# Second product of the attention over the block means in one piece per head, another warm-up, and another list of pieces for the start of a fused kernel

## The chip, the cores and the metric

The kernel runs on one core of a Trainium2 chip. The metric is the device time of one execution in microseconds (us), the median of three runs. The engines are TensorE (PE, with PEld for its weight loads), VectorE (DVE), ScalarE (ACT), GpSimd (POOL) and SyncE (SP, which issues the DMAs here).

## What is computed

Three layers run one behind the other on 3072 tokens (4 sequences of 768) of 512 numbers (8 heads of 64). The first is attention in which each query sees the keys less than 16 positions away, and one summary for each block of 32 keys (the maximum of the keys, the mean of the values):

```python
k_sum = k.reshape(B, H, nb, block, D).max(axis=3)
v_sum = v.reshape(B, H, nb, block, D).mean(axis=3)
scores_l = where(|q_pos - k_pos| < 16, scale * q @ k.T, -1e9)
scores_s = scale * q @ k_sum.T + np.log(block)
a = softmax(concat[scores_l, scores_s])
x = a @ concat[v, v_sum]            # then as 3072 x 512
h = x @ w_in                        # 512 -> 2048
g = h * np.cos(h)
x = g @ w_out                       # 2048 -> 512
# then a soft mixture of 8 experts of 4 slots each over all tokens
logits = x @ phi
slot_out[e] = maximum((softmax(logits, 0).T @ x)[e] @ w1[e], 0) @ w2[e]
out = softmax(logits, 1) @ slot_out
```

## The kernel before

The attention works on 24 groups: a group is 256 queries of four heads, in two parts j of two heads (hh) and four blocks u of 64 queries. A block of 64 queries sees KL = 96 keys and NSUM = 24 summaries, so a row of scores S has 120 numbers. For the first four groups (0 to 3, the first 512 tokens) the pieces of a part are: `sc` (scores on PE, L327 against the keys, L330 against the key summaries that `u`, L199, has reduced), `ev` and `mx` (mask and row maximum on DVE, L336 and L344), `ex` (exponentials on ACT, L366), `nm` and `nt` (normalisation, L449, L451, L456), `tr` and `aT` (transposition on PE, L469, and copy out of PSUM on ACT or DVE, L479), and the two products with the values: `av` over the 96 keys and `aw` over the 24 means, both through `first_x` with one product of 64 columns for each block and head (L520). The means `vs` are made on PE (L215) out of the loads `vb`. Then `xh` and `xl` (L536, L540) split x into two halves of a fast PE format.

The second layer runs in 96 slots: 6 blocks of 512 tokens by 16 blocks of 128 of the 2048 inner columns. A slot has twelve products into h (L580, L581, L588), then `p`, `q` (DVE, L600, L604), `n` (the sine on ACT, L608), `r` (DVE, L618) and the split of g (L622, L631); two slots later its products into the output sums (L652 to L675). In the first 16 slots the weights come by DMA (`W`, the buffers raw) and are converted: `ca`, `cb` on ACT (L134, L139), `cc` on DVE (L148), `cd` on POOL (L156), and their high and low halves (L553, L560). The raw buffers of the weights are single: a load waits for the conversion of the weights two before it. The loads of the keys from the fifth pair on share one buffer (`v2`), so each waits for the reduction `u` of the one before. SP has at most eight DMAs under way.

All pieces up to slot 80 are recorded under names by `do`, and `emit` issues them in the order of the hand list `ORDER` on all five engines: an engine meets its instructions in the order in which the list names them, and waits at each for what it needs. `fill` (L895) records products of a matrix of ones (L902, warmth), whose result nobody reads: in the list f1 and f11 stand at the start and f21 and f31 further down, ten products of 128 columns each. After slot 80 only PE and SP are ordered by hand.

Of the kernel before, what the change touches and what calls it, by code (L numbers as in the profile page):

```python
# [23 lines left out]
QB = 64  # L24
NQ = S // QB
WIN, SUMB = 16, 32
KL = QB + 2 * WIN
NSUM = S // SUMB
KC = KL + NSUM
# [6 lines left out]
NFILL = 40  # L36
F0 = 10
# [36 lines left out]
def body(ctx: ExitStack, tc: tile.TileContext, q0, qk, kT, vT, vn, vx, w, phi, ex, cst, out):  # L74
    nc = tc.nc
# [18 lines left out]
    def do(name, fn, *a):  # L94

        if not waiting:
            return fn(*a)
        assert name not in pieces, name
        pieces[name] = (fn, a)
        queue.append(name)  # L100
# [3 lines left out]
    NM = 6 * KC  # L104
    mask = att.tile([128, 6, KC], F32, name="mask", tag="mask", bufs=1)
    ident = const.tile([128, 128], F32, name="ident")
# [4 lines left out]
    ones = const.tile([128, 128], F32, name="ones")  # L111
# [47 lines left out]
    ksums, vsums, grp = {}, {}, {}  # L159
# [6 lines left out]
    def bank(name):  # L166
        pool, tag = place_of[name]
        return pool.tile([128, 512], F32, name=name, tag=tag)
# [33 lines left out]
    def load_vb(b, i):  # L202
        do(f"b{b}_{i}", load_vb_, b, i)
# [46 lines left out]
    def vsum_first():  # L250

        reserve("vs0")
        for i in range(3):
            do(f"vs0_{i}", vsum_f, i)
        do("vt0", vsum_g)
# [158 lines left out]
    def att_exp(pair):  # L414
        do(f"ae{pair}", att_exp_, pair)
# [66 lines left out]
    def att_D(g):  # L482
        if g < 4:
            reserve(f"av{g}")
            for j in range(2):
                do(f"av{g}_{j}", first_av, g, j)
                do(f"aw{g}_{j}", first_aw, g, j)
        else:
            do(f"av{g}", att_av, g, (0, 1))
        do(f"xh{g}", att_xh, g)  # L490
        do(f"xl{g}", att_xl, g)

    def att_av(g, js):
        d = grp[g]
        if "av" not in d:
            d["av"] = bank(f"av{g}") if g < 4 else ps_m.tile([128, 512], F32, name=f"av{g}", tag="m")
        ps = d["av"]
        for j in js:
            for u in range(4):
                c = 256 * j + QB * u  # L500
                for hh in range(2):
                    r = slice(64 * hh, 64 * hh + 64)
                    a = d["aT", j][:, 128 * u + 64 * hh:] if g < 4 else d["aT", hh][:, 256 * j + 64 * u:]
                    nc.tensor.matmul(ps[r, c:c + QB], d["v"][:KC, j, u, r], a[:, 0:QB], start=True, stop=True)  # L504

    def first_av(g, j):
        first_x(g, j, grp[g]["v"][:KL, j], slice(0, KL))

    def first_aw(g, j):
        p = 2 * (g % 2) + j  # L510
        first_x(g, j, vsums[0][KL:KC, p:p + 1, :].to_broadcast([NSUM, 4, 128]), slice(KL, KC))

    def first_x(g, j, v, k):
        d = grp[g]
        if "av" not in d:
            d["av"], d["parts"] = bank(f"av{g}"), 0
        for u in range(4):
            for hh in range(2):
                r = slice(64 * hh, 64 * hh + 64)
                nc.tensor.matmul(d["av"][r, 256 * j + QB * u:256 * j + QB * u + QB], v[:, u, r],  # L520
                                 d["aT", j][k, 128 * u + 64 * hh:128 * u + 64 * hh + QB],
                                 start=d["parts"] == 0 and u == 0, stop=d["parts"] == 3 and u == 3)
        d["parts"] += 1

    def att_x(g):
        b, o = g // 4, 256 * ((g // 2) % 2)
        if b not in xh:
            xh[b] = xres.tile([128, 4, TB], F32R, name=f"xh{b}", tag="xh", bufs=2)
            xl[b] = xres.tile([128, 4, TB], F32R, name=f"xl{b}", tag="xl", bufs=2)
        p = 2 * (g % 2)  # L530
        hi, lo = (x[b][:, p:p + 2, o:o + 256] for x in (xh, xl))
        return hi, lo, grp[g]["av"].rearrange("p (j c) -> p j c", j=2)

    def att_xh(g):
        hi, lo, ps = att_x(g)
        nc.scalar.copy(hi, ps)  # L536
# [8 lines left out]
    def split_w(f, part, eng=None, s=None):  # L545
        nm = "io"[part]
        do(f"{nm}h{f if s is None else s}", split_hi, f, part)
        do(f"{nm}l{f if s is None else s}", split_lo, f, part, eng)
# [344 lines left out]
    warmth = ps_h.tile([128, 512], F32, name="warmth", tag="h")  # L893

    def fill(n):  # L895

        for i in range(0, n, 10):
            do(f"f{i + (n > F0)}", fill_, min(10, n - i))

    def fill_(n):  # L900
        for i in range(n):
            nc.tensor.matmul(warmth[:, 0:128], ones, ones, start=True, stop=True)  # L902
# [5 lines left out]

    def load_mask2(_):
        do("N", load_mask2_)  # L910

    def load_mask2_():
        nonlocal mask2
        mask2 = att.tile([128, 6, KC], F32, name="mask2", tag="mask", bufs=1)
        nc.sync.dma_start(out=mask2[:, 0:4, :].rearrange("p w c -> p (w c)"), in_=cst[:, NM + 468:NM + 468 + 4 * KC])

    mask2 = None

    C = lambda t, o, n: (lambda _: do(f"C{o}", lambda: nc.sync.dma_start(out=t, in_=cst[:, o:o + n])))
    todo = dict(F=lambda _: fill(F0), f=lambda _: fill(NFILL), I=C(ident, NM, 128), M=C(mask.rearrange("p w c -> p (w c)"), 0, NM),  # L920
                A=C(avg, NM + 128, 52), S=C(sel, NM + 180, 288), N=load_mask2, P=lambda _: do("P", lambda: nc.sync.dma_start(out=phis.rearrange("p k s -> p (k s)"), in_=phi)),
                K=load_kraw, Q=load_q_first, W=load_w, B=lambda i: load_vb(0, i), V=load_v, G=load_qk, X=load_vs,
                k=ksum, s=scores, e=exps, v=lambda _: vsum_first(), t=turn, d=att_D, c=convert, c1=conv_1,
                w=lambda f: split_w(f, 0), a=att_K)
    for token in PRE.split():
        n = token.lstrip("FfIMNASPKQWBVGXksevtdcwa")
        todo[token[:len(token) - len(n)]](int(n or 0))


    def late_exp(pair):  # L930
        with tc.issue_after(turn_dve["sin"].ins):
            att_exp(pair)
# [7 lines left out]
    for g in range(4, 24):  # L940
        h0 = HF[g // 2 % 2] + 2 * NF * (g // 4 - 1) if g > 7 else HB[g // 2 % 2]
        h = h0 + OA * (g % 2)
        n = h0 + ON + DN * (g % 2)
        if g < 8:
# [4 lines left out]
            c = n + OC  # L949
            at2(c + OD, att_D, g)  # L950
        else:
            v = n - 14 + OD2
# [3 lines left out]
            c = n + OC2  # L956
# [16 lines left out]
    for b in range(1, B):  # L973
        s = 8 * (3 * b - 2) - 4
        for i in range(8):
            load, use, k = (load_kraw, ksum, 4 * b + i) if i < 4 else (load_vraw, vadd, 4 * b + i - 4)
# [31 lines left out]
    for f in range(NPRE, NF):  # L1008
        c = max(f - CL, 0)
# [9 lines left out]
    def emit():  # L1019
        nonlocal waiting  # L1020
        waiting = False
        names = ORDER.split() or queue
        assert sorted(names) == sorted(queue), set(names) ^ set(queue)
# [329 lines left out]
```

## Time and profile before

| | us |
|---|---|
| median of three runs | 727.8 (727.47 to 728.17) |
| profiled execution | 730.21 |
| span of that execution in the trace | 728.4 |
| PE busy | 711.3 (98% of the span) |
| DVE, ACT, POOL busy | 435.8, 411.5, 406.9 |
| PE's share of the chain that ended last | 92% |

The trace is of one execution: times in it are us from the start of its span, and 1.8 us of the execution lie around the span. Busy time is what an engine spends in instructions; "idle before" an instruction has the one that it waited for behind an arrow, or "issue" where the trace shows none. PEclk is the clock that TensorE was granted, as a share of its full speed. The ends of products on PE are modelled, so that neighbouring rows overlap by some hundredths of a microsecond; a product of 32-bit numbers is two records.

### The profile page before, as it was taken

The numbers are of one execution on the slowest core, as the hardware profiler recorded it, in microseconds if no ns is written. First come the engines' busy times: TensorE is split into PE (matmuls) and PEld (weight loads), VectorE is DVE, ScalarE is ACT, GpSimd is POOL, SyncE is SP. The second block draws the span as 40 slices with busy tenths as digits, with TensorE's granted clock in tenths as the row PEclk, the third lists the DMA queues.
The fourth block names the chain that finished last, engine by engine and source line by source line (L and its number), as shares of the span: only waits on it lengthen the run. The fifth ranks groups of instructions, "written<-read, shape, count | busy, mean of one in ns | idle before, by whom it ended". The sixth has DMA issues, their size and how long they took to land.

```text
span 728.4 us, 13277 instructions
## 1 busy us (share of the span) xinstructions
PE 711.3 (98%) x5260; PEld 560.0 (77%) x5260; DVE 435.8 (60%) x680; ACT 411.5 (56%) x772; POOL 406.9 (56%) x310
## 2 busy tenths in 40 slices
PE   9899999999999999999999999999999999999994
PEld 9878777788887887787888787888787887787453
DVE  5678986974676574776574754674953444334323
ACT  4789997565554654654654754564735445434113
POOL 0756857766465565565673666674577665762000
PEclk9899999999999999999999999999999999999998
DMA  9976856402212301401302201301302822227998
GB/s 345 398 281 249 301 212 230 166 22 76 92 67 77 112 1 54 140 24 43 111 1 74 80 0 35 116 1 43 117 1 87 318 87 87 94 95 269 410 370 295
DMA packets 34862, 101.65 MB, mean 140 GB/s; under 512 B 3440, under 2 KB 13936, under 8 KB 32752
## 3 DMA queue, kind: packets, MB, share of 16 engines
q1 hardware_dynamic: 34800, 100.81, 38.1%
q8 instruction: 41, 0.67, 0.4%
q14 instruction: 21, 0.17, 0.1%
HBM read 92.54 MB, written 6.29 MB: 136 GB/s over the span
## 4 chain that ended last, share of the span: by engine, by line
PE 92%; ACT 4%; DVE 2%; issue 1%; POOL 0%
PE h L580 12%; PE h L581 12%; PE h L588 12%; PE acc L666 10%; PE acc L675 10%; PE acc L667 10%; PE tr L469 3%; PE av L504 3%; PE sc L384 2%; PE acc L652 2%; PE acc L653 2%; PE acc L655 2%; PE yp L1219 2%; PE hp L1173 2%; PE warmth L902 2%; PE av L520 1%
## 5 line engine op out<-in xcount | busy, mean ns | idle before, releaser
L631 POOL TENSOR_TENSOR gl<-a,gh 128x512 fp32r<-128x512 f32 x96 | 129.1, 1345 | 120.4 <-ACT gh L622 62.8
L560 POOL TENSOR_TENSOR wol<-w,woh 128x512 fp32r<-128x512 f32 x96 | 126.4, 1318 | 65.4 <-ACT woh L553 64.1
L580 PE MATMUL h<-xh,wih 128*128 128x512 f32 x384 | 155.4, 405 | 2.8 <-DVE a L618 2.8
L581 PE MATMUL h<-xl,wih 128*128 128x512 f32 x384 | 152.7, 398 | 0.0
L600 DVE TENSOR_SCALAR a<-h 128x512 f32<-128x512 f32 x96 | 66.0, 688 | 128.8 <-PE h L588 76.9
L608 ACT ACTIVATE a<-a,halfpi 128x512 f32<-128x512 f32 x96 | 69.4, 724 | 110.1 <-DVE a L604 109.8
L666 PE MATMUL acc<-woh,gh 128*128 128x512 f32 x320 | 127.4, 398 | 0.0
L667 PE MATMUL acc<-wol,gh 128*128 128x512 f32 x320 | 125.4, 392 | 0.0
L560 POOL TENSOR_TENSOR wil<-w,wih 128x512 fp32r<-128x512 f32 x81 | 106.9, 1323 | 30.0 <-PE h L588 11.4
L588 PE MATMUL h<-xh,wil 128*128 128x512 f32 x384 | 106.8, 401 | 0.0
L618 DVE TENSOR_TENSOR a<-h,a 128x512 f32<-128x512 f32 x96 | 65.9, 688 | 50.1 <-ACT a L608 50.1
L580 PEld LDWEIGHTS h<-xh,wih 128*128 128x128 f32 x384 | 72.3, 188 | 23.1 <-issue 3.7
L675 PE MATMUL acc<-woh,gl 128*128 128x512 f32 x320 | 88.3, 397 | 0.0
L581 PEld LDWEIGHTS h<-xl,wih 128*128 128x128 f32 x384 | 72.5, 189 | 16.0 <-DVE xl L540 0.5
L588 PEld LDWEIGHTS h<-xh,wil 128*128 128x128 f32 x384 | 71.0, 189 | 16.7 <-issue 1.0
L553 ACT CAST woh<-w 128x512 fp32r<-128x512 f32 x96 | 59.4, 619 | 32.1 <-PE acc L675 25.1
L553 ACT CAST wih<-w 128x512 fp32r<-128x512 f32 x96 | 59.3, 618 | 25.2 <-PE h L581 23.1
L622 ACT CAST gh<-a 128x512 fp32r<-128x512 f32 x96 | 58.9, 617 | 24.5 <-PE acc L667 19.1
L666 PEld LDWEIGHTS acc<-woh,gh 128*128 128x128 f32 x320 | 60.1, 188 | 14.4 <-issue 1.3
L667 PEld LDWEIGHTS acc<-wol,gh 128*128 128x128 f32 x320 | 60.2, 188 | 12.9
L675 PEld LDWEIGHTS acc<-woh,gl 128*128 128x128 f32 x320 | 58.8, 188 | 13.1 <-issue 0.6
L604 DVE SCALAR_TENSOR_TENSOR a<-a,h 128x512 f32<-128x512 f32 x96 | 65.5, 682 | 2.2
(156 smaller groups left out, 962.3 us busy)
## 6 DMA issues: line engine op xcount, KB each, us to landing
ex<-in_ex_dram SPq DMA_DIRECT2D x64, 512.0 KB
raw<-in_w_dram SPq DMA_DIRECT2D x16, 1024.0 KB
qk<-in_qk_dram SPq DMA_DIRECT2D x20, 736.0 KB
v<-in_vx_dram SPq DMA_DIRECT2D x24, 512.0 KB
kr<-in_kT_dram SPq DMA_DIRECT2D x16, 384.0 KB
out_dram<-o SPq DMA_DIRECT2D x12, 512.0 KB
vr<-in_vT_dram SPq DMA_DIRECT2D x12, 384.0 KB
v<-vs SPq DMA_DIRECT2D x40, 48.0 KB
```

The lines of the kernel that those rows point to most:

```text
L553: nc.scalar.copy(hi, W[f][:, part, :])
L560: (eng or nc.gpsimd).tensor_tensor(out=lo, in0=W[f][:, part, :], in1=hi, op=ALU.subtract)
L580: nc.tensor.matmul(h, hi[:, c], xh[s // NF][:, t, :], start=t == 0, stop=False)
L581: nc.tensor.matmul(h, hi[:, c], xl[s // NF][:, t, :], start=False, stop=False)
L588: nc.tensor.matmul(h, lo[:, c], xh[s // NF][:, t, :], start=False, stop=t == 3)
L600: nc.vector.tensor_scalar(out=a, in0=h, scalar1=0.25, scalar2=MAGIC, op0=ALU.add, op1=ALU.add)
L608: turn_dve["sin"] = nc.scalar.activation(a, a, AF.Sin, bias=halfpi, scale=-TWO_PI)
L618: nc.vector.tensor_tensor(out=a, in0=h, in1=a, op=ALU.mult)
L631: nc.gpsimd.tensor_tensor(out=gl, in0=a, in1=gh, op=ALU.subtract)
L666: nc.tensor.matmul(acc[t], gh[:, c], hi, start=f == 0, stop=False)
L667: nc.tensor.matmul(acc[t], gh[:, c], lo, start=False, stop=False)
L675: nc.tensor.matmul(acc[t], gl[:, c], hi, start=False, stop=f == NF - 1)
```

## The change

Three things are changed. The second product `aw` takes the four query blocks u of a head at once: two products of 256 columns for a part (one per head) in place of eight of 64, with the transposed probabilities read in strides; there are 16 of them in place of 64. The flags that begin and end the sum follow. The warm-up is four products of 512 columns, three in f0 and one in f1, both at the start, in place of forty of 128 columns, twenty of them further down. And the list `ORDER` is made anew, with 1927 names in place of 1929; the rules that it keeps (what waits for what) are the same. Lines up to 520 stand two lower in the new file.

```diff
-NFILL = 40
-F0 = 10
-ORDER = """kz1 kz3 kz2 kz0 K0 f1 Q0 Q2 K1 C0 Q1 f11 K3 C720 u0 C848 K2 sc0_0 W0 sc2_0 u1 K4 Q3 ev0_0 sc0_1
+ORDER = """zz1 kz0 kz3 kz2 kz1 K0 f0 Q0 K1 C0 C848 Q2 K2 Q1 u0 C720 K3 f1 W0 u1 sc0_0 V0 Q3 sc0_1 ev0_0 b0_0
...
     def first_av(g, j):
-        first_x(g, j, grp[g]["v"][:KL, j], slice(0, KL))
-
-    def first_aw(g, j):
-        p = 2 * (g % 2) + j
-        first_x(g, j, vsums[0][KL:KC, p:p + 1, :].to_broadcast([NSUM, 4, 128]), slice(KL, KC))
-
-    def first_x(g, j, v, k):
         d = grp[g]
         if "av" not in d:
             d["av"], d["parts"] = bank(f"av{g}"), 0
+        d["parts"] += 1
         for u in range(4):
             for hh in range(2):
                 r = slice(64 * hh, 64 * hh + 64)
-                nc.tensor.matmul(d["av"][r, 256 * j + QB * u:256 * j + QB * u + QB], v[:, u, r],
-                                 d["aT", j][k, 128 * u + 64 * hh:128 * u + 64 * hh + QB],
-                                 start=d["parts"] == 0 and u == 0, stop=d["parts"] == 3 and u == 3)
+                nc.tensor.matmul(d["av"][r, 256 * j + QB * u:256 * j + QB * u + QB], d["v"][:KL, j, u, r],
+                                 d["aT", j][:KL, 128 * u + 64 * hh:128 * u + 64 * hh + QB],
+                                 start=d["parts"] == 1 and u == 0, stop=False)
+
+    def first_aw(g, j):
+        d = grp[g]
         d["parts"] += 1
+        for hh in range(2):
+            r = slice(64 * hh, 64 * hh + 64)
+            a = d["aT", j][KL:KC, :].rearrange("p (u h c) -> p u h c", u=4, h=2)[:, :, hh, :]
+            nc.tensor.matmul(d["av"][r, 256 * j:256 * j + 256].rearrange("p (u c) -> p u c", u=4),
+                             vsums[0][KL:KC, 2 * (g % 2) + j, r], a, start=False, stop=d["parts"] == 4)
...
     def fill(n):
-
-        for i in range(0, n, 10):
-            do(f"f{i + (n > F0)}", fill_, min(10, n - i))
+        for i, k in enumerate((3,1,)):
+            do(f"f{i}", fill_, k)
 
     def fill_(n):
-        for i in range(n):
-            nc.tensor.matmul(warmth[:, 0:128], ones, ones, start=True, stop=True)
+        for _ in range(n):
+            nc.tensor.matmul(warmth, ones, ones.unsqueeze(1).to_broadcast([128, 4, 128]), start=True, stop=True)
```

What the list moves is seen in the order of the instructions on an engine. On PE, behind the scores of the first four groups: vs are the means of the values, vb a load that they are made of, aT the transposed probabilities of a group and part, v its values, av the sums, tr a transposition of the probabilities S. Before, the three means stand in a row and the products behind them:

```order
L469 MATMUL tr2_0_422<-ident_88,S2_208 120x128 x4
L215 MATMUL vs0_428<-vb0_0_204,avg_90 32x128 x8
L215 MATMUL vs0_428<-vb0_1_231,avg_90 32x128 x8
L215 MATMUL vs0_428<-vb0_2_227,avg_90 32x128 x8
L520 MATMUL av2_460<-aT2_0_439,v2_237 64x64 x8
L520 MATMUL av2_460<-aT2_1_457,v2_237 64x64 x8
L520 MATMUL av0_486<-aT0_0_391,v0_284 64x64 x8
L520 MATMUL av2_460<-aT2_1_457,vs0_471 64x64 x8
```

And in the new list:

```order
L213 MATMUL vs0_353<-vb0_0_173,avg_90 32x128 x8
L467 MATMUL tr0_1_363<-ident_88,S0_171 120x128 x4
L213 MATMUL vs0_353<-vb0_1_194,avg_90 32x128 x8
L213 MATMUL vs0_353<-vb0_2_200,avg_90 32x128 x8
L512 MATMUL av0_402<-aT0_0_388,v0_150 64x64 x8
L467 MATMUL tr2_0_421<-ident_88,S2_224 120x128 x4
L467 MATMUL tr2_1_427<-ident_88,S2_224 120x128 x4
L522 MATMUL av0_402<-aT0_0_388,vs0_416 64x256 x2
L512 MATMUL av2_442<-aT2_0_434,v2_226 64x64 x8
```

Group 0 comes ahead of group 2, transpositions stand between the products, and the second product is two instructions where it was eight.

On SP, the loads from the first weights on (raw0 to raw4 are the weights, kr the keys, q queries, vb and v values). Before:

```order
L126 DMA raw0_160<-in_w_dram 128x2048
L191 DMA kr4_181<-in_kT_dram 128x768
L273 DMA q3_183<-in_q0_dram 128x512
L208 DMA vb0_0_204<-in_vn_dram 128x2x512
L126 DMA raw1_223<-in_w_dram 128x2048
L208 DMA vb0_2_227<-in_vn_dram 128x2x512
L208 DMA vb0_1_231<-in_vn_dram 128x2x512
L290 DMA v2_237<-in_vx_dram 128x1024
L290 DMA v0_284<-in_vx_dram 128x1024
L191 DMA kr5_387<-in_kT_dram 128x768
L290 DMA v1_389<-in_vx_dram 128x1024
L126 DMA raw2_395<-in_w_dram 128x2048
```

And in the new list:

```order
L124 DMA raw0_129<-in_w_dram 128x2048
L288 DMA v0_150<-in_vx_dram 128x1024
L271 DMA q3_152<-in_q0_dram 128x512
L206 DMA vb0_0_173<-in_vn_dram 128x2x512
L206 DMA vb0_1_194<-in_vn_dram 128x2x512
L206 DMA vb0_2_200<-in_vn_dram 128x2x512
L288 DMA v1_222<-in_vx_dram 128x1024
L288 DMA v2_226<-in_vx_dram 128x1024
L124 DMA raw1_264<-in_w_dram 128x2048
L288 DMA v3_287<-in_vx_dram 128x1024
L189 DMA kr4_292<-in_kT_dram 128x768
L124 DMA raw2_322<-in_w_dram 128x2048
```

The four loads of v stand ahead of the load of the fifth keys, kr4, and raw1 stands behind three of them.

On DVE around the tenth slot (sm and rs are the normalisation of an attention group, S its scores, a8 and a9 the slots' intermediate results). Before:

```order
L148 TENSOR_SCALAR w11_1244<-w11_1244 128x1024
L449 TENSOR_SCALAR sm7_1350<-sm7_1350 128x8
L451 RECIPROCAL rs7_1381<-sm7_1350 128x8
L199 TENSOR_REDUCE ks9_1384<-kr9_1313 128x24
L604 SCALAR_TENSOR_TENSOR a9_1355<-a9_1355,h9_1272 128x512
L618 TENSOR_TENSOR a8_1332<-h8_1226,a8_1332 128x512
```

And in the new list:

```order
L146 TENSOR_SCALAR w11_1193<-w11_1193 128x1024
L600 TENSOR_SCALAR a9_1296<-h9_1195 128x512
L604 SCALAR_TENSOR_TENSOR a9_1296<-a9_1296,h9_1195 128x512
L618 TENSOR_TENSOR a8_1270<-h8_1142,a8_1270 128x512
L447 TENSOR_SCALAR sm7_1256<-sm7_1256 128x8
L449 RECIPROCAL rs7_1321<-sm7_1256 128x8
```

The step L618 of slot 8 stands ahead of the normalisation of group 7 instead of behind it, and the key reduction is no longer between them.

## Rows read from the trace of the kernel before

**Rows 1.** Windows: stretch, us; busy us (instructions) of each engine; PEclk, DMA share, GB/s.
```profile
109.00:660.00 551.00, 550.55 (x3560) 438.67 (x3559) 328.02 (x498) 300.21 (x508) 341.01 (x262) 1.00 0.23 82
80.00:103.00 23.00, 23.00 (x186) 18.15 (x185) 20.62 (x32) 22.76 (x57) 17.92 (x10) 1.00 0.73 263
103.00:109.00 6.00, 4.19 (x12) 3.12 (x11) 5.43 (x8) 5.45 (x9) 2.56 (x2) 0.72 0.51 194
33.30:37.00 3.70, 3.70 (x20) 3.33 (x20) 1.38 (x2) 3.49 (x6) 1.34 (x2) 0.50 0.99 405
713.00:719.30 6.30, 5.11 (x36) 3.63 (x28) 3.75 (x7) 3.39 (x7) 0.00 (x0) 1.00 0.94 316
```

**Rows 2.** PE's timeline, 0 to 42 us: start, us, instruction, count [idle before, releaser].
```profile
1.08 7.31 PE L902 MATMUL warmth<-ones 128*128 128x128 f32 x40 [1.08 <-DVE ones L113]
...
11.82 2.50 PE L902 MATMUL warmth<-ones 128*128 128x128 f32 x20
...
20.48 2.40 PE L902 MATMUL warmth<-ones 128*128 128x128 f32 x20
...
27.23 1.03 PE L520 MATMUL av<-aT,vs 24*64 24x64 f32 x28
30.16 1.14 PE L520 MATMUL av<-aT,vs 24*64 24x64 f32 x20 [1.90 <-issue]
...
33.33 3.67 PE L469 MATMUL tr<-ident,S 128*120 128x128 f32 x16
36.93 2.22 PE L520 MATMUL av<-aT,v 96*64 96x64 f32 x64
39.08 2.08 PE L520 MATMUL av<-aT,vs 24*64 24x64 f32 x64
41.09 0.50 PE L580 MATMUL h<-xh,wih 128*128 128x512 f32 x1
```

**Rows 3.** ACT's waits and DVE's groups of instructions, 0 to 49 us.
```profile
ACT S L366 <- DVE mx L344: 9.3, 2, 8.8
ACT xh L536 <- PE av L520: 6.1, 4, 2.3
...
L199 DVE TENSOR_REDUCE ks<-kr 128x24 f32<-128x768 f32 x7 | 6.5, 934 | 5.5 <-DMA kr<-in_kT_dram 5.5
L336 DVE SCALAR_TENSOR_TENSOR S<-sc,mask 128x480 f32<-128x480 f32 x8 | 5.2, 646 | 2.1 <-PE sc L330 2.1
```

**Rows 4.** ACT's timeline: the first exponential, the first sine, what follows it.
```profile
11.06 0.40 ACT L366 ACTIVATE S<-S,mx 128x120 f32<-128x120 f32 x1 [8.84 <-DVE mx L344]
...
48.10 0.73 ACT L608 ACTIVATE a<-a,halfpi 128x512 f32<-128x512 f32 x1
48.73 0.60 ACT L553 CAST woh<-w 128x512 fp32r<-128x512 f32 x1
```

**Rows 5.** PE's timeline in the last stage: products of 256 columns, and a wait.
```profile
692.68 3.64 PE L1219 MATMUL yp<-ex,hT 128*32 128x256 f32 x64
...
715.43 1.69 PE L1254 MATMUL op<-so,cT 128*128 128x256 f32 x12 [0.92 <-DVE so L1242]
```

**Rows 6.** DMA, 0 to 37 us: the sum, and the loads of weights.
```profile
DMA packets 4215, 13.76 MB, mean 372 GB/s; under 512 B 542, under 2 KB 670, under 8 KB 3570
...
raw<-in_w_dram SPq DMA_DIRECT2D x5, 1024.0 KB
```

**Rows 7.** Timelines of ACT, DVE and PE around the tenth slot.
```profile
101.64 0.72 ACT L608 ACTIVATE a<-a,halfpi 128x512 f32<-128x512 f32 x1
...
100.36 2.32 DVE L449 TENSOR_SCALAR sm<-sm 128x8 f32<-128x8 f32 x1 [0.17 <-ACT S L438]
...
103.65 0.68 DVE L604 SCALAR_TENSOR_TENSOR a<-a,h 128x512 f32<-128x512 f32 x1
104.25 0.68 DVE L618 TENSOR_TENSOR a<-h,a 128x512 f32<-128x512 f32 x1
...
105.08 0.47 PE L580 MATMUL h<-xh,wih 128*128 128x512 f32 x1 [1.81 <-DVE a L618]
```

More of the change, by code (lines that the diff above doesn't have):

```diff
@@ L919, in body @@
     C = lambda t, o, n: (lambda _: do(f"C{o}", lambda: nc.sync.dma_start(out=t, in_=cst[:, o:o + n])))
-    todo = dict(F=lambda _: fill(F0), f=lambda _: fill(NFILL), I=C(ident, NM, 128), M=C(mask.rearrange("p w c -> p (w c)"), 0, NM),
+    todo = dict(f=lambda _: fill(0), I=C(ident, NM, 128), M=C(mask.rearrange("p w c -> p (w c)"), 0, NM),
                 A=C(avg, NM + 128, 52), S=C(sel, NM + 180, 288), N=load_mask2, P=lambda _: do("P", lambda: nc.sync.dma_start(out=phis.rearrange("p k s -> p (k s)"), in_=phi)),
```

2 lines of the change are left out of this document (1 added, 1 removed).

## The prediction

> **What bounds the kernel now.** I began with the windows over stages [rows 1]. From 109 to 660 us TensorE (PE) is busy 550.55 of 551.00 us at a granted clock of 1.00: nothing in the change alters the products of that stretch, so it only starts earlier or later, and whatever the start gains reaches the end one for one. In 80 to 103 us both PE (23.00 of 23.00) and ScalarE (ACT, 22.76 of 23.00) are full. What can be won lies before the first slots of the second layer run, and at one hole at 103 to 109, where PE is busy 4.19 of 6.00 us at 0.72.
>
> The timeline of PE [rows 2] shows the losses of the start: warm-up products at 1.08, at 11.82 and at 20.48; an idle gap of 1.90 us ahead of 30.16 in which PE waited for nothing that the trace shows; then a clock of 0.50 (33.3 to 37.0 in [rows 1]) and the first product of h at 41.09. ACT's waits [rows 3] show who suffers: it waits 6.1 us, four times, for the last products of av before it can cast x (L536). And the timeline of ACT [rows 4] shows where the two meet: its first exponential starts at 11.06 and the first sine of a slot, which every later slot stands behind, at 48.10. Between these ACT has 37.04 us, of which it waits the 6.1 and 0.5 (9.3 in all for maxima, less the 8.84 ahead of the first exponential); so it has 30.4 us of work there and is the chain that I follow.
>
> **The change part by part.** Warm-up at the start: 40 records took 7.31 us, and at the full clock 20 take 2.50 or 2.40, so about .12 us each. 40 of them would be 4.8; the 2.5 us more are some 21 records at half the clock. Now there are 8 records of four times the columns: 21 slow short ones (5.04 us) are 5.25 long ones, the other 2.75 take .48 each, 1.3 us; the sum is 6.4, so they end at 7.4 to 7.5 instead of 8.39. Bounds are 4.9 (all fast) and 8.8 (all slow); I take -0.9 for the first score and so for the first exponential, 10.1 to 10.2.
>
> Warm-up in the middle: two bundles of 2.4 to 2.5 us leave PE, 4.8 in all. PE carried them in front of work that ACT then waited for, so they were not hidden.
>
> Second product of av: four pieces of 16 records took 2.08 us [rows 2], .52 a piece. Now a piece has four records of 256 columns. Nearest is the row of yp, 64 records of 256 columns in tiles of 32 columns, four side by side, in 3.64 us [rows 5]: .228 for a bundle. If the two halves run side by side, a piece is two bundles, .46; if they don't, it is four, .91. Eight pieces: -0.5 to +3.1 us; I take -0.5, since the old pieces' halves already ran faster than one after another would allow. It lies beside ACT's work and hardly touches the sum.
>
> The row at 27.23 starts with the tile size changed from the one before, and 64 records of av from 36.93 to 39.08 are followed by the 64 of the second product with no gap. The Trainium skill, "TensorEngine Tiling (Array Packing)", section "Tiling Modes" (Key Properties), says that a change of tiling mode drains TensorE; the new list groups second products into four runs where there were three, two changes more, which speaks against it. The trace agrees only up to what is lost in the overlap of neighbouring rows, about 0.1 us each: by that rule the sum would be 0.2 us worse at most.
>
> The list. Every load of v now stands ahead of the fifth key load and of the third weight load in SP's queue, where the fifth key load held the queue for the buffer of a reduction before. I see no price in the four v loads coming first but one: the fourth and fifth weight loads. The start moved 13.76 MB in 37 us with DMA all but full (share 0.99 [rows 1], mean 372 GB/s [rows 6]); summed along SP's new queue the fourth weight load ends at 12.1 MB and the fifth at 13.1, by that rate at 32.5 and 35.3 us, and since up to eight loads are under way and share the engines I take 35 and 38; behind the fifth stand two conversions, a cast, the table load and the sine. ACT would like to be there earlier. The chain by hand: PE's scores end sooner by 0.9, but the third key reduction now stands behind six mask and maximum steps of .64 (3.9 us from the first score at 8.6, to 12.5; then .93 [rows 3]), while PE has done its four pieces of 1.14 ((11.82-8.39)/3 [rows 2]) at 12.0: PE waits about 1.4 us there. Without fills, without the 1.90 gap and at full clock, the remaining products end, and h starts, at about 33.4 instead of 41.09: 0.9+4.8+1.9+3.4 (half of the 6.8 us from 30.16 to 36.93)+0.5 = 11.5, less 1.4 at the scores and some 2.4 for transposes and copies that PE now catches up with. So PE comes 7.7 us earlier and no longer binds ACT; the 6.1 us go, and weight loads come next. For ACT: -0.9 (start), -6.1 (waits for av), +0.5 (the cast of the first output weights, behind the sine at 48.73 before, stands ahead of it now), +1.0 for the new waits (between 0.2, when the loads are just in time, and 4, when they lag). That is -5.5: the first sine at 42.6, and no part before 103 us that could give more.
>
> At 103 to 105 PE waits 1.81 us for the last step of slot 8's g on VectorE (L618, [rows 7]). ACT's sine started at 101.64, but VectorE was in a normalisation (2.32 us from 100.36, most of it waiting), a reciprocal, a reduction of keys and a multiply of slot 9 before it took that step at 104.25. In the new list the step stands ahead of the normalisation and the reduction; it can start when the sine has ended, at 102.3, near 1.4 us of the wait earlier after the two multiplies that remain ahead of it. I take -1.4, bounds 0 (the sine itself is late) and -1.8. The clock there fell to 0.72 for 6 us, 1.7 us of work lost; I don't count that as gained, because PE now reaches the second slot long before the first sine and will wait about 2 us for it there, and both gaps of that length in this trace (1.90 and 1.81) were followed by a fall, while 0.92 us ahead of 715.43 was not [rows 1, 5].
>
> Sum: -5.5-1.4 = -6.9, from 730.21 to 723.3 for a profiled execution. That execution lay 2.4 us above the median of 727.8, so the median to expect is **720.9**.
>
> **Rivals.** (a) The clock falls once in the prologue: the 1.4 us wait at the third reduction lies between the 0.92 that cost nothing and the 1.81 that did. Then PE does some 6.8 us of products at half the clock again, 3.4 us, of which the weight loads hide 1: +2.4, 723.3. (b) It falls nowhere, not at the second slot either, the hole at 103 goes whole and the loads are in time: 0.9+6.1-0.5+1.81+1.7 = 10.0, 717.8. (c) The loads lag: the last two weight blocks come 3 us later than reckoned since the v loads went ahead of them: 723.9. (d) Slower: the two fills of 2.4 us kept PE busy where scores and transposes leave gaps. If without them the clock is at half from about 12 us on, the products up to h (33.4-12.0, less the 3.8 of waits above: 17.6 us) take twice that; less 2.2 of waits filled, h starts near 48.8, 7.6 us later than before, and the median is 731 to 735. It decides if PEclk is below 0.7 over 12 to 30 us. What speaks for it is the half clock after 30 us; what speaks against is that ahead of it PE had been idle for 1.90 us and that the fills before it ran at the full clock. (e) The list does nothing for the end: PE starts earlier but ACT, full from 80 to 103, is refilled by the work that the list has put there, 727 to 728.
>
> **How the numbers follow.** The forecast (719.3 to 722.5) has .38, (a) .21, (b) .14, (c) .12, (d) .09, (e) .06. The range 717.0 to 726.5 takes in all of the first four with the bounds of the second product and of the loads. A difference of 0.2%, 1.5 us, is about what a measurement of this kernel can tell from none: faster .84, same .07, slower .09.
>
> **What would show it.** First exponential at about 10.1 and first sine near 42.6 (41.5 to 43.5); ACT's wait for av ahead of the casts of x under 1.5 us in all; h from about 33.4; the wait at the slot that now stands at 98 us under 0.6; PEclk near 1.00 from 8 to 33; 551 us for the stretch from there as before. Wrong would be: a first sine later than 46, half clock before 30 us, a mean of over .4 us for records of the second product, or a hole of PE in 45 to 100 that the old trace doesn't have.

## The result, and the profile after

The changed kernel takes 719.98 us (median of 4 runs, 718.54 to 721.71) where the kernel before takes 727.98 in the same comparison; the ratio is 0.9876, 95% interval 0.9828 to 0.9924. Run once more beside other kernels it took 718.98 (718.58 to 720.41), ratio 0.9897 (0.9872 to 0.9922). The prediction was 720.9, and its range holds the time.

One execution of this kernel says less than one would like. Over all comparisons the kernel before took 724.6 to 732.9 us, so differences below are given as ratios with their intervals, and a trace shows where time goes in one execution, not how often.

The profiled execution took 720.45 us with a span of 718.7, that is 9.8 us less than that of before (730.21; 728.4). PE's timeline of the changed kernel answers to [rows 2]; start in the span, duration, instruction, count, and in brackets the idle time before it and what ended that:

```profile
1.09 6.60 PE L901 MATMUL warmth<-ones 128*128 128x512 f32 x8 [1.09 <-DVE ones L111]
...
23.45 0.65 PE L522 MATMUL av<-aT,vs 24*64 24x256 f32 x4
24.73 1.62 PE L512 MATMUL av<-aT,v 96*64 96x64 f32 x48 [0.63 <-DVE aT L477]
26.27 1.08 PE L522 MATMUL av<-aT,vs 24*64 24x256 f32 x8
27.29 3.56 PE L467 MATMUL tr<-ident,S 128*120 128x128 f32 x16
30.78 0.67 PE L522 MATMUL av<-aT,vs 24*64 24x256 f32 x4
31.37 2.08 PE L512 MATMUL av<-aT,v 96*64 96x64 f32 x64
33.39 1.94 PE L522 MATMUL av<-aT,vs 24*64 24x256 f32 x16
35.26 0.50 PE L580 MATMUL h<-xh,wih 128*128 128x512 f32 x1
```

The fills and the gap of 1.90 us with no releaser are gone, and h starts at 35.26 instead of 41.09. PE's waits up to 110 us (engine and line, what it waited for, us in all, times, longest):

```profile
PE sc L328 <- DVE ks L197: 1.2, 1, 1.2
PE warmth L901 <- DVE ones L111: 1.1, 1, 1.1
PE h L580 <- DVE a L618: 1.0, 1, 1.0
PE av L512 <- DVE aT L477: 0.6, 1, 0.6
PE av L512 <- PE vs L213: 0.5, 1, 0.5
```

ACT's waits up to 49 us and its first exponential and first sine, answering to [rows 3, 4]:

```profile
ACT S L364 <- DVE mx L342: 8.1, 1, 8.1
ACT aT L477 <- PE tr L467: 1.1, 1, 1.1
```

```profile
10.35 0.39 ACT L364 ACTIVATE S<-S,mx 128x120 f32<-128x120 f32 x1 [8.12 <-DVE mx L342]
...
42.14 0.72 ACT L608 ACTIVATE a<-a,halfpi 128x512 f32<-128x512 f32 x1
```

ACT no longer waits for av (6.1 us before). The windows, as in [rows 1] (stretch, us, busy time and instructions of PE, PEld, DVE, ACT, POOL, granted clock, DMA share, GB/s):

```profile
27.40:30.80 3.40, 3.40 (x18) 3.06 (x18) 3.21 (x5) 2.36 (x4) 3.12 (x3) 0.51 1.01 419
97.00:103.00 6.00, 6.00 (x55) 4.72 (x53) 5.67 (x8) 5.02 (x8) 4.14 (x3) 1.00 0.32 114
103.00:109.00 6.00, 6.00 (x30) 4.93 (x29) 3.73 (x7) 5.50 (x9) 4.97 (x3) 1.00 0.94 352
109.00:651.00 542.00, 541.57 (x3493) 432.56 (x3492) 326.91 (x491) 293.00 (x498) 340.19 (x258) 1.00 0.22 79
```

Between 8 and 109 us there is half a clock once, for the sixteen transpositions at 27.3. The hole at the tenth slot, whose h now starts at 97.15, is closed: PE is busy 6.00 of 6.00 us at 1.00 both from 97 to 103 and from 103 to 109, where before it was 4.19 of 6.00 at 0.72 from 103. From the first sine to the end of the span it took 680.3 us before (728.4 less 48.10) and 676.6 now (718.7 less 42.14). So of the 9.7 us of the span 6.0 came ahead of the first sine and 3.7 behind it, which is about the hole's 1.81 and the half clock's 1.7.

### The profile page after: what moved, and what is told of

Read it like the earlier page. It is cut to its first block, busy times and chain, and to the rows that moved or that the text cites. A ratio compares the mean times of both kernels' runs of the same rounds, so it can differ in the third digit from the quotient of the medians.

```text
span 718.7 us, 12965 instructions
## 1 busy us (share of the span) xinstructions
PE 702.8 (98%) x5092; PEld 547.3 (76%) x5092; DVE 439.4 (61%) x680; ACT 409.7 (57%) x772; POOL 412.3 (57%) x310
## 4 chain that ended last, share of the span: by engine, by line
PE 94%; DVE 4%; ACT 1%; issue 0%; DVEq 0%; ACTq 0%
PE h L580 13%; PE h L581 12%; PE h L588 12%; PE acc L666 10%; PE acc L675 10%; PE acc L667 10%; PE tr L467 3%; PE av L502 3%; PE sc L382 3%; PE acc L652 2%; PE acc L653 2%; PE acc L655 2%; PE yp L1218 2%; PE hp L1172 2%; PE xt L712 1%; PE warmth L901 1%
## 5 line engine op out<-in xcount | busy, mean ns | idle before, releaser
L631 POOL TENSOR_TENSOR gl<-a,gh 128x512 fp32r<-128x512 f32 x96 | 131.0, 1366 | 114.5 <-ACT gh L622 69.1
L560 POOL TENSOR_TENSOR wil<-w,wih 128x512 fp32r<-128x512 f32 x81 | 108.6, 1346 | 16.9 <-ACT wih L553 8.9
L588 PE MATMUL h<-xh,wil 128*128 128x512 f32 x384 | 105.1, 399 | 0.0
L618 DVE TENSOR_TENSOR a<-h,a 128x512 f32<-128x512 f32 x96 | 65.7, 687 | 43.8 <-ACT a L608 43.6
```

Of the source, the lines that this page charges most:

```text
L560: (eng or nc.gpsimd).tensor_tensor(out=lo, in0=W[f][:, part, :], in1=hi, op=ALU.subtract)
L588: nc.tensor.matmul(h, lo[:, c], xh[s // NF][:, t, :], start=False, stop=t == 3)
L618: nc.vector.tensor_tensor(out=a, in0=h, in1=a, op=ALU.mult)
L631: nc.gpsimd.tensor_tensor(out=gl, in0=a, in1=gh, op=ALU.subtract)
```

## The experiments

### What the second product is worth, and why

The kernel before with the new second product alone:

```diff
-        first_x(g, j, vsums[0][KL:KC, p:p + 1, :].to_broadcast([NSUM, 4, 128]), slice(KL, KC))
+        d = grp[g]
+        if "av" not in d:
+            d["av"], d["parts"] = bank(f"av{g}"), 0
+        for hh in range(2):
+            r = slice(64 * hh, 64 * hh + 64)
+            a = d["aT", j][KL:KC, :].rearrange("p (u h c) -> p u h c", u=4, h=2)[:, :, hh, :]
+            nc.tensor.matmul(d["av"][r, 256 * j:256 * j + 256].rearrange("p (u c) -> p u c", u=4),
+                             vsums[0][KL:KC, p, r], a, start=d["parts"] == 0, stop=d["parts"] == 3)
+        d["parts"] += 1
```

> The kernel before with the new second product of av alone (two products of 256 columns in place of eight of 64 for a part; list and warm-up as before). Theory now: PE's gap ahead of the 963rd of its instructions (weight loads and products counted, the 64-column pieces use some 130 in 2.1 us) is the supply of instructions, 256 at a time, which falls behind where 256 are used up in about 4 us; with 96 products and 96 weight loads fewer there is no such gap, and no half clock behind it: first h 3 to 5 us earlier, 2.5 to 5 us below the kernel before. Rival (the prediction's): the product itself is worth 0.5 us and lies beside ScalarE's chain, within 0.7 us of before.

Measured: 725.92 us, ratio to before 0.9969 (0.9940 to 0.9997), 2.3 us less where 2.5 to 5 were expected; the interval alone (0.2 to 4.4 us) does not exclude the rival's 0.7, the trace does. The start did what the theory said: PE has no gap there any more and a clock of 1.00 all through, and the first sine starts 6.3 us earlier than in the trace of before. But only 4.1 of these 6.3 us reached the end of that execution (a span of 724.3 against 728.4). Windows, then timelines of ACT and PE:

```profile
25.00:30.00 5.00, 5.00 (x90) 3.78 (x87) 4.28 (x10) 4.51 (x14) 3.93 (x4) 1.00 1.03 422
30.00:35.00 5.00, 5.00 (x90) 3.91 (x89) 2.69 (x5) 4.51 (x8) 5.00 (x4) 1.00 1.01 418
...
97.00:103.00 6.00, 2.84 (x7) 2.29 (x8) 5.48 (x9) 5.72 (x10) 3.18 (x3) 0.76 0.63 221
```

```profile
41.77 0.73 ACT L616 ACTIVATE a<-a,halfpi 128x512 f32<-128x512 f32 x1
...
95.70 1.28 ACT L616 ACT_TABLE_LOAD   x1
97.00 0.72 ACT L616 ACTIVATE a<-a,halfpi 128x512 f32<-128x512 f32 x1
```

```profile
100.16 0.76 PE L588 MATMUL h<-xh,wih 128*128 128x512 f32 x1 [3.21 <-DVE a L626]
```

The hole at the tenth slot has grown from 1.81 to 3.21 us (lines from 520 on have numbers eight higher in this file), since the list there is as before: sixteen exponentials and a table load stand ahead of the slot's sine on ACT, whenever PE comes.

The reverse, the changed kernel with the old second product:

```diff
-        for hh in range(2):
-            r = slice(64 * hh, 64 * hh + 64)
-            a = d["aT", j][KL:KC, :].rearrange("p (u h c) -> p u h c", u=4, h=2)[:, :, hh, :]
-            nc.tensor.matmul(d["av"][r, 256 * j:256 * j + 256].rearrange("p (u c) -> p u c", u=4),
-                             vsums[0][KL:KC, 2 * (g % 2) + j, r], a, start=False, stop=d["parts"] == 4)
+        for u in range(4):
+            for hh in range(2):
+                r = slice(64 * hh, 64 * hh + 64)
+                nc.tensor.matmul(d["av"][r, 256 * j + QB * u:256 * j + QB * u + QB], vsums[0][KL:KC, 2 * (g % 2) + j, r],
+                                 d["aT", j][KL:KC, 128 * u + 64 * hh:128 * u + 64 * hh + QB],
+                                 start=False, stop=d["parts"] == 4 and u == 3)
```

> The changed kernel with the second product of av as before, eight products of 64 columns for a part in place of two of 256. Theory: the two forms cost PE about the same (0.3 to 0.6 us in all eight pieces), beside ScalarE's chain: within 0.7 us of the changed kernel. Rival: the long form is what brings PE forward, 2 us or more above the changed kernel; or the long form costs more, 1 to 3 us below it.

Measured: 724.89 us, ratio to before 0.9932 (0.9905 to 0.9959), so above the changed kernel by 4.9 to 5.9 us between the medians and 2.5 to 4.1 between the ratios (the intervals overlap a little, but its fastest run, 723.09, is slower than the slowest of the changed kernel, 721.71); this theory, the prediction's, fell, and the rival that the long form brings PE forward stands. PE's timeline shows that it isn't by the time of the products themselves: up to the first h the rows are those of the changed kernel within 0.15 us each.

```profile
30.76 0.68 PE L522 MATMUL av<-aT,vs 24*64 24x64 f32 x16
31.37 2.09 PE L512 MATMUL av<-aT,v 96*64 96x64 f32 x64
33.38 2.08 PE L522 MATMUL av<-aT,vs 24*64 24x64 f32 x64
...
37.34 0.54 PE L581 MATMUL h<-xh,wih 128*128 128x512 f32 x1 [1.88 <-ACT w L132]
```

```profile
37.30:40.50 3.20, 3.16 (x8) 2.50 (x8) 1.29 (x2) 1.06 (x1) 2.06 (x1) 0.52 0.70 247
```

PE stops for 1.88 us ahead of its first h and then runs at half the clock. The releaser named (a conversion of weights on ACT) is nothing that this product reads; the casts of x that it needs were done. So it is the gap of before in another place, and the question is what sets its place. I counted all of PE's records from the start of the trace up to every such gap: weight loads, products, and the 8 to 16 semaphore and drain instructions of its sequencer (without these the counts are 695 to 697, 949 to 953 and 1201 to 1207). The last column is how long a transfer of instructions, of which more below, had landed when PE went on:

| kernel | records before the gap | gap, us | landed before, us |
|---|---|---|---|
| before; with L618 moved (below) | 962; 962 | 1.90; 0.81 | 1.40; 1.44 |
| before, new warm-up (below) | 1218 | 1.08 | 1.47 |
| changed, old second product | 1218 | 1.88 | 1.28 |
| changed, old product, 18 small products more | 962 | 0.25 | 1.52 |
| changed, old product, warm-up of 20 | 706 and 962 | 1.49 and 0.43 | 1.44 and 1.48 |
| changed, fills in the gaps (below) | 706 | 0.39 | 1.61 |

To a record, 706, 962 and 1218 are 256 apart. Two runs moved this border on purpose. The first puts useless products in a gap:

```diff
-u2 ex2_0_0 nm0 sc1_0
+u2 ex2_0_0 nm0 f2 sc1_0
...
+        do("f2", fill_s, 18)
...
+            nc.tensor.matmul(warmth[:, 0:8], ones, ones[:, 0:8], start=True, stop=True)
```

> The changed kernel with the old second product of av, and 18 useless products of 8 columns (72 instructions of PE) in the 1.2 us in which PE waits for the third key reduction. Theory: they move the border between two blocks of 256 instructions from the first product of h, where the 256 before it took 4.0 us, to a place where the 256 before it take 6.9 us, so the gap of 1.9 us there and the half clock behind it go although PE has more to do: 2.5 to 4.5 us below the kernel with the old product without them. Rival: the gap belongs to the place in the program (a wait for the casts of x), and the useless products change nothing or cost up to 1 us.

Measured: 725.05 us, ratio 0.9967 (0.9945 to 0.9990): no gain. The gap at the first h did go, and one of 0.25 us stands at record 962. But the probe was not cheap: the 36 records took 4.63 us where I had meant them to take 1.2, and the clock fell while they ran: 0.80 from 12 to 16 us is 1.6 us at half, so the fall came at 14.4, and they end at 15.5. PE's timeline and windows:

```profile
10.85 4.63 PE L903 MATMUL warmth<-ones 128*128 128x8 f32 x36
...
31.71 0.37 PE L522 MATMUL av<-aT,vs 24*64 24x64 f32 x2 [0.25 <-issue]
```

```profile
12.00:16.00 4.00, 4.00 (x38) 3.98 (x37) 2.03 (x5) 3.12 (x12) 1.79 (x1) 0.80 0.99 392
16.00:21.00 5.00, 5.00 (x66) 4.61 (x66) 2.94 (x5) 2.67 (x12) 0.69 (x1) 0.50 1.06 419
```

So its time decides nothing, its place of the gap does. The second moves the border by 64 records with no work in the middle:

```diff
-K3 f1 W0
+K3 W0
...
-        for i, k in enumerate((3,1,)):
-            do(f"f{i}", fill_, k)
+        do("f0", fill_, 20)
...
-            nc.tensor.matmul(warmth, ones, ones.unsqueeze(1).to_broadcast([128, 4, 128]), start=True, stop=True)
+            nc.tensor.matmul(warmth[:, 0:128], ones, ones, start=True, stop=True)
```

> The changed kernel with the old second product of av and a warm-up of 20 products of 128 columns in place of four of 512: 64 instructions more of PE, all at the start, and 0 to 0.8 us more of its time there. Theory: the border between two blocks of 256 instructions moves 64 instructions ahead, from the first product of h to the second products before it, where the 256 ahead of it took 6.9 us and not 4.0; the gap of 1.9 us at the first h and the half clock behind it go: 1.5 to 4 us below the kernel with the old product alone (724.9). Rival: the gap belongs to the place in the program and stays: no difference, or up to 0.8 us above.

Measured: 721.59 us (8 runs), 3.3 below the kernel with the old product and the short warm-up between the medians, but only 1.2 between the ratios to before (0.9916, 0.9886 to 0.9945, against 0.9932, 0.9905 to 0.9959); the intervals overlap, so the gain is likely and not certain. The profiled execution is the longest of the eight (727.11, the others 720.7 to 722.2) and shows why one execution isn't enough: the gap at the first h is gone, but two others stand at borders, and the clock is 0.56 from 30 to 35 us and 0.50 from 35 to 42.

```profile
23.48 0.41 PE L213 MATMUL vs<-vb,avg 128*32 128x128 f32 x4 [1.49 <-issue]
...
29.98 2.66 PE L467 MATMUL tr<-ident,S 128*120 128x128 f32 x14 [0.43 <-issue]
```

What this settles: the gap stands only at places 256 records apart, not at each of them, wherever they fall in the program, and goes with the number of instructions, not with a wait of the kernel. What PE waits for there is in the traces too: the transfers of instructions have a queue of their own, q8 (transfers, MB, share of the 16 DMA engines; the kernel before, then the changed one):

```profile
q8 instruction: 41, 0.67, 0.4%
...
q8 instruction: 40, 0.66, 0.4%
```

They are of 16 KB each, one for every 256 of PE's 10617 and 10294 records. In the trace of before one runs from 27.82 to 28.76 us, and PE goes on at 30.16, 1.40 later. At all eight gaps it is 1.3 to 1.6 us from the landing of such a transfer to PE's next product (the table's last column). At every later border up to 110 us without such a gap the transfer had landed 1.6 us or more before; only the first border, 194, has none ahead of it. So the gap is the supply of instructions coming late. At the eight gaps the transfer started 2.8 to 4.8 us after PE had passed the border before and took 0.9 to 1.1, so that PE went on 5.3 to 7.2 us after that border, although it had used up the 256 records in 4.1 to 6.3 us. The Trainium skill, "Runtime: NRT & Kernel Launch", section "Instruction fetch mechanics", says that an engine's instructions are refilled in blocks of 256, which agrees with the 256 here, and that crossing a border is mostly hidden, which these rows do not bear out: 0.25 to 1.90 us each, while the DMA share is about 1.0. What remains open is why a transfer starts 2.8 us after a border in one execution and 4.8 in another: record 706 costs 1.49 us in the one with the late start, and nothing in most.

### The warm-up

The kernel before with the new warm-up alone:

```diff
-K0 f1 Q0
+K0 f0 Q0
...
-Q1 f11 K3
+Q1 f1 K3
...
-ex0_0_1 f21 W1
+ex0_0_1 W1
...
-nt2 f31 mx3_1
+nt2 mx3_1
...
-        for i in range(0, n, 10):
-            do(f"f{i + (n > F0)}", fill_, min(10, n - i))
+        for i, k in enumerate((3,1,)):
+            do(f"f{i}", fill_, k)
...
-            nc.tensor.matmul(warmth[:, 0:128], ones, ones, start=True, stop=True)
+            nc.tensor.matmul(warmth, ones, ones.unsqueeze(1).to_broadcast([128, 4, 128]), start=True, stop=True)
```

> The kernel before with the new warm-up alone: four products of 512 columns at the start, the two bundles of ten at 11.82 and 20.48 taken out, nothing else moved. Theory: the fills stood ahead of work that ScalarE waits for, so that most of their 4.8 us comes off its 6.1 us of waits: first exponential 0.7 earlier, first sine 3 to 5 us earlier, the time 2.5 to 5 less than before. Rival: the fills held the clock, and without them PE runs at half the clock between 12 and 30 us: 0 to 7 us more than before.

Measured: 725.0 us, ratio 0.9956 (0.9928 to 0.9984), 3.2 to 4.1 us less, as expected. In its trace the first exponential starts at 10.05 and the first sine at 42.00, with a clock of 1.00 from 8 to 35 us (the gap of 1.08 us of the table and half a clock come after that), so what rival (d) of the prediction reckons with does not show: the fills were not what held the clock there. The hole at the tenth slot is there as before:

```profile
42.00 0.72 ACT L608 ACTIVATE a<-a,halfpi 128x512 f32<-128x512 f32 x1
...
101.28 0.47 PE L580 MATMUL h<-xh,wih 128*128 128x512 f32 x1 [1.80 <-DVE a L618]
```

And the changed kernel with the two bundles put back:

```diff
-mx0_1 sc2_1
+mx0_1 f2 sc2_1
...
-tr0_0 mx1_0
+tr0_0 f3 mx1_0
...
+        for i in (2, 3):
+            do(f"f{i}", fill_s, 10)
...
+            nc.tensor.matmul(warmth[:, 0:128], ones, ones, start=True, stop=True)
```

> The changed kernel with the two bundles of ten warm-up products of 128 columns that the kernel before had, behind the third piece of scores and behind the first transposition. Theory: PE starts its h 2.5 to 4.5 us later, ScalarE waits for it again and the first sine comes 2 to 3.5 us later: 1.5 to 3.5 us above the changed kernel. Rival: the bundles fill waits and keep the clock up, within 1 us of it.

Measured: 722.73 us, ratio 0.9911 (0.9883 to 0.9939), above the changed kernel by 2.7 to 3.8 us between the medians and 1.0 to 2.5 between the ratios, about as expected (the intervals overlap). First h at 36.52, first sine at 43.38, clock 1.00 from 20 to 50 us: they kept the clock up and were still too dear.

### What the list is worth

Both product edits on the list of before, so that only the list is missing: the edit of the kernel before with the second product alone (above), and the edit of its warm-up, whose part in the list is:

```diff
-K0 f1 Q0
+K0 f0 Q0
...
-Q1 f11 K3
+Q1 f1 K3
...
-ex0_0_1 f21 W1
+ex0_0_1 W1
...
-nt2 f31 mx3_1
+nt2 mx3_1
...
```

> The kernel before with both edits of products, the second product of av of 256 columns and the new warm-up, on the list of before without its two fills. Theory: the start gains what the changed kernel's does (first sine at 40.5 to 42.5, no gap, no half clock), but the hole at the tenth slot grows by what PE comes earlier, since the exponentials and the table load ahead of that slot's sine don't move, from 1.8 to 3 us or more: 722.5 to 726, that is 2 to 5 us below before and 3 to 6 above the changed kernel, which is the new list's share. Rival: the list adds nothing beyond the start, 718 to 721.

Measured: 721.64 us, ratio 0.9905 (0.9868 to 0.9942). That is below what either edit gives alone (0.9969 and 0.9956) and above the changed kernel by 1.7 to 2.7 us between the medians and 0.6 to 2.1 between the ratios. The theory had the hole at the tenth slot at 3 us or more and the time at 722.5 or above; the profiled execution has 0.85:

```profile
99.00 0.47 PE L588 MATMUL h<-xh,wih 128*128 128x512 f32 x1 [0.85 <-DVE a L626]
```

So the hole isn't simply what PE comes earlier by, and how large it is in other executions is not shown. Nor was the start that of the changed kernel: on the old list PE waits 1.57 us for the third key reduction and 1.30 for a normalisation on GpSimd, the clock is 0.86 from 8 to 20 us and 0.84 and 0.82 in the two stretches from 25 to 35, and the first sine stands at 42.81. The list's own share is thus some 2 us, and not clear of the scatter.

The one move at the tenth slot that the prediction spoke of, alone on the list of before:

```diff
-nt6 m7a ax7_3 cc11 nm7 cd11 u9 tr6_0 n8 q9 tr6_1 K10 ih10 G8 m7b r8 oh8
+nt6 m7a ax7_3 cc11 cd11 tr6_0 n8 q9 tr6_1 ih10 G8 m7b r8 nm7 u9 K10 oh8
```

> The kernel before with one edit of its list: the last step of slot 8's g (L618 on VectorE) ahead of the normalisation of group 7, the key reduction and the key load that follows it. Theory: the hole of 1.81 us at slot 10 closes and with it goes the fall of the clock behind it (1.7 us), so 3.0 to 3.6 us less than before, with PE full and PEclk 1.00 from 100 to 109. Rival: only the wait goes and the clock falls all the same, 1.4 to 1.8 less. Second rival: another wait of the same size comes next, no difference.

Measured: 726.89 us, ratio 0.9962 (0.9940 to 0.9983), 2.2 to 2.8 us less where 3.0 to 3.6 were expected. The hole shrank only to 1.39, since VectorE now waits 1.80 us for the sine:

```profile
101.81 0.69 DVE L618 TENSOR_TENSOR a<-h,a 128x512 f32<-128x512 f32 x1 [1.80 <-ACT a L608]
```

```profile
102.65 0.47 PE L580 MATMUL h<-xh,wih 128*128 128x512 f32 x1 [1.39 <-DVE sm L449]
```

and the clock did not fall behind it (PEclk 1.00 from 97 to 109). Up to that place this kernel is the one before, instruction for instruction, and yet its first sine stood at 46.09 and not 48.10 (first exponential at 10.29 instead of 11.06, gap 0.81 instead of 1.90): two microseconds between two executions of the same code. The reverse edit on the changed kernel:

```diff
-cc11 m7a p9 cd11 q9 n8 tr6_0 ih10 tr6_1 r8 aT6_0 m7b nm7 il10
+cc11 m7a p9 nm7 cd11 u9 q9 n8 tr6_0 ih10 tr6_1 r8 aT6_0 m7b il10
...
-oh8 u9 cb12
+oh8 cb12
```

> The changed kernel with one edit of its list: the normalisation of group 7 and the key reduction ahead of the last step of slot 8's g on VectorE, as before. Theory: the hole at slot 10 comes back, 1 to 1.8 us and a fall of the clock behind it, 2.5 to 3.5 us above the changed kernel. Rival: the place of that step is not what made the hole, within 0.5 us of the changed kernel.

Measured: 721.23 us, ratio 0.9893 (0.9863 to 0.9924). The hole is back, with no fall of the clock, and the time 1.2 to 2.2 us above the changed kernel's medians, less than expected, while the ratios of the two don't differ by more than their intervals:

```profile
96.81 0.47 PE L580 MATMUL h<-xh,wih 128*128 128x512 f32 x1 [1.33 <-DVE a L618]
```

### What is left at the start

The changed kernel a second time:

> The changed kernel once more, nothing edited, as the measure for the runs beside it: both theories expect the time of the changed kernel, 718.5 to 722, first sine at 41 to 43, no gap of PE over 1.3 us between 10 and 109.

Measured: 718.98 us. In this execution the sixteen transpositions ran at the full clock and the first sine stood at 40.95, 1.2 us earlier than in the first trace (the first exponential at 9.83, 0.5 earlier):

```profile
27.43 1.96 PE L467 MATMUL tr<-ident,S 128*120 128x128 f32 x16
```

Fills in the gaps that are left, to hold that clock:

```diff
-nm0 sc1_0
+nm0 f2 sc1_0
...
-ex3_0_0 av0_0
+ex3_0_0 f3 av0_0
...
-ex3_0_1 av2_0
+ex3_0_1 f4 av2_0
...
+        for i, k in ((2, 4), (3, 1), (4, 2)):
+            do(f"f{i}", fill_s, k)
...
+            nc.tensor.matmul(warmth[:, 0:128], ones, ones, start=True, stop=True)
```

> The changed kernel with warm-up products of 128 columns in three of PE's gaps of the start: four in that of 1.2 us, one in that of 0.5, two in that of 0.6. Theory: they keep the clock up at 27.4 to 30.8 us, so the transpositions there take 2.0 and not 3.6 us and ScalarE's wait of 1.1 us for them goes: first sine up to 1 us earlier, 0.5 to 1.2 us below the changed kernel. Rival: the fall there is hidden behind the loads, no difference; or the fills come late and cost up to 1 us.

Measured: 719.51 us (718.90 to 719.74), ratio 0.9871 (0.9841 to 0.9902): no difference to the changed kernel. The clock stayed up and the first sine came at 40.55, but PE then waited elsewhere:

```profile
27.40:30.80 3.40, 3.40 (x62) 2.85 (x61) 3.25 (x6) 3.40 (x7) 2.82 (x2) 1.00 1.05 437
```

```profile
71.38 0.47 PE L580 MATMUL h<-xh,wih 128*128 128x512 f32 x1 [0.56 <-DVE a L618]
```

And the first sine ahead of the conversions of the fifth weights:

```diff
-cd3 W5 h1a ca4 p0 q0 cb4 u5 sc4 W6 cc4 K6 h1c il2 V4 cd4 n0 V5 ev4_0 C900 y5_1 r0 ih3
+cd3 W5 h1a p0 q0 n0 r0 ca4 cb4 u5 sc4 W6 cc4 K6 h1c il2 V4 cd4 V5 ev4_0 C900 y5_1 ih3
```

> The changed kernel with the first slot's sine (and its two steps of VectorE before, one behind) ahead of ScalarE's conversions of the fifth weights in the list. Theory: ScalarE's work, not a load, sets the first sine at 42.1; two conversions of 2.2 us stand ahead of it that can come later, so it starts near 40 and PE's wait of 1.03 us at the third slot goes: 0.8 to 1.1 us below the changed kernel. Rival: the conversions come late for the fifth slot instead, and the wait turns up there; no difference, or up to 1 us above.

Measured: 721.25 us, ratio 0.9923 (0.9899 to 0.9946), about 2 us above the changed kernel beside it. The sine came at 40.10, and the wait turned up twice further on, as the rival said, though at more than its 1 us. A part may be the clock: this trace has the fall at 27.3 (0.73 from 25 to 30 us) that the changed kernel's trace beside it has not.

```profile
47.65 0.50 PE L580 MATMUL h<-xh,wih 128*128 128x512 f32 x1 [1.12 <-DVE a L618]
52.36 0.50 PE L580 MATMUL h<-xh,wih 128*128 128x512 f32 x1 [0.75 <-DVE a L618]
```

## Why the prediction was right, and where it was not

The time and the chain were right; two terms were not what they were said to be.

- **ACT as the chain.** Right. First exponential 10.35, and 9.83 in the second trace (forecast 10.1 to 10.2), no wait for av, first sine 42.14 (forecast 42.6). In the profiled execution -5.96 where the sum had -5.5.
- **Warm-up at the start.** Right: it ends at 7.69, said 7.4 to 7.5. So is the half clock that the working has there: in the trace of before the records start 0.21 us apart up to 6.4 us and 0.11 behind that. The clock column prints 1.00 for that stretch, but the trace's first record of the clock is at 6.53, so the column says nothing ahead of it. In the two traces of the changed kernel that record stands at 6.96 and 5.54, and the first exponential at 10.35 and 9.83: a scatter of over half of the 0.9 us taken.
- **Fills.** Right, and now measured: 0.9956 for taking them out of the old list, 1.0 to 3.8 us for putting them back. The condition of rival (d), a clock below 0.7 over 12 to 30 us, was not met: in the changed kernel's first trace it was 1.00 up to 27.4.
- **Second product.** The term failed. A piece takes 1.94/4, 0.48 us, near the 0.46 taken; but "lies beside ACT's work and hardly touches the sum" is wrong. Its worth is 96 records of products and 96 weight loads fewer ahead of the border between blocks of instructions. The 1.90 us gap and the half clock behind it, 5.3 of the 11.5 us by which the working brought h forward, were counted as gone with no cause named for it; the runs with the old product put back (gap of 1.88, 2.5 to 5.9 us) and with a moved border show what it hangs on. That they did go is luck as far as the prediction is concerned: with the old product, which it put within 0.5 us of the new one, they stay and the kernel takes 724.89.
- **h at 33.4.** It came at 35.26, since the clock fell for 3.4 us at 27.4, against the sign of a clock near 1.00 from 8 to 33, and at 33.79 in the second trace, where it didn't. One fall in the start is rival (a), but not behind the wait that it names: that one, 1.23 us at 13.74, had none, and ahead of 27.4 the waits were 0.47 and 0.63 us. The price was 1.1 us of ACT's time (its wait for the transpositions), not 2.4: other ACT work lay beside it.
- **New waits.** Taken at 1.0: 1.2 us at the third key reduction on PE (1.4 said), 1.1 on ACT for transpositions; 0.6 for a weight load in the second trace. Rival (c) did not occur.
- **Tenth slot.** Mis-sized: -1.4 taken, about -3.5 measured (the hole of 1.81 whole, and the 1.7 of the clock). Two steps of it failed. The place of L618 is not enough: moved alone, it leaves 1.39, as the sine ends late (the bound 0 that the prediction named); in the changed kernel the sine stands at 95.07 behind its table load and PE has other work until then. And the clock that was to fall instead where PE waits for the first sine did not: PE waited 1.03 us there, not 2, and PEclk stayed 1.00.
- **Rival (e)** did not occur in the changed kernel, but there is something in it: a part of the gain of the start can be swallowed at the tenth slot. On the old list the trace of the new product alone shows that, with a hole of 3.21 us.
- **Tile changes.** Four runs of second products instead of three show no loss: the neighbouring rows at 26.27 and 33.39 overlap as those of before do, so the 0.2 us that the prediction allowed for are not to be seen.

The sum for the profiled execution was 6.9 us and 9.8 were measured; against the medians, 8.0 or 9.2 us (719.98 and 718.98 against 727.98 and 728.22).

## What to carry to other kernels

Where a gap on an engine has no releaser, count its instructions up to it in two or three versions before you count the gap as gone, and set it beside the transfers of instructions: here such gaps stand at places 256 records apart where a transfer landed late, and fewer, longer instructions were worth more than their own time. A gain ahead of a stage reaches the end only if the next hole behind it isn't set by another engine: look for that hole and ask whether it grows. And where two executions of the same code differ by more than the term, one trace a side can't size the term.

## What the runs showed of the hardware that I had not expected

- PE's gaps with no releaser, or with one that the product does not read, stood only at records 706, 962 and 1218, 256 apart, in the traces of seven kernels, and cost 0.25 to 1.90 us. Each ended 1.3 to 1.6 us after a transfer of 16 KB of instructions had landed.
- 36 records of 8 columns took 4.63 us, 0.129 each, no less than records of 128 columns (20 in 2.40 to 2.50 us). And the granted clock fell to 0.50 at their end though PE shows as busy throughout.
- How long PE had been idle did not tell whether its clock fell: 1.39, 1.33 and 1.80 us (ahead of 102.65, 96.81 and 101.28 in three kernels) had no fall behind them, 1.81, 1.88 and 3.21 had one, and so had 0.81 (PEclk 0.50 at 30 to 35 in the kernel with L618 moved).
